# Linear attention and a mixture of experts on one core: query rows copied by DMA and transposed through an fp32r view, tail keys stacked, and a new order table

## The chip, the core and the metric

The kernel runs on one core of a Trainium2 chip. Its engines are TensorE (PE; its weight loads are listed apart as PEld), VectorE (DVE), ScalarE (ACT), GpSimd (POOL) and SyncE (SP), which here only issues DMAs. Each engine works through its own instructions in the order in which they stand; semaphores hold an instruction back until its operands are there. The metric is device time in microseconds for one execution, the median of several.

## The reference

For every batch and head, queries and keys are projected to 128 features, shifted by the row's largest absolute value, and turned into 256 features by exp(x) and exp(-x). Linear attention follows, and then one expert of eight for each token (4608 tokens of 512 numbers):

```python
def phi(x):
    proj = np.einsum('bhsd,df->bhsf', x, w_phi)
    proj = proj - np.max(np.abs(proj), axis=-1, keepdims=True)
    return np.concatenate([np.exp(proj), np.exp(-proj)], axis=-1)
q_p, k_p = (phi(q), phi(k))
kv = np.einsum('bhsf,bhsd->bhfd', k_p, v)
z = np.sum(k_p, axis=2)
num = np.einsum('bhsf,bhfd->bhsd', q_p, kv)
den = np.einsum('bhsf,bhf->bhs', q_p, z)[..., None] + 1e-06
attn = num / den                      # 8 batches, 8 heads, 576 rows, 64 columns
...
logits = x @ w_gate                   # x: attn as 4608 tokens x 512
expert_idx = np.argmax(logits, axis=1)
...
h = np.maximum(xe @ w1[e], 0.0)       # the tokens xe of expert e
out[mask] = gate_w[mask, None] * (h @ w2[e])
```

## The kernel before

**Units.** Attention runs in 16 units. A unit holds two batches (`bb`) and two heads (`hh`). The 576 rows of a batch are four chunks of 128 rows and a tail of 64; the tails of the two batches share chunk 8, batch 0 in partitions 0 to 63 and batch 1 in 64 to 127. `PIECES` (line 208) is the order of the chunks in a unit.

**Precision.** Products that must be exact to fp32 are made of fp32r operands split in two: a high part (`xh`, `kh`, `vh`, `wh`, `hh`) and the low rest (`xl`, `kl`, `vl`, `wl`, `hl`). Three matmuls, high by high, low by high, high by low, give one product. ScalarE mostly makes the high parts, VectorE and GpSimd the low ones.

**The steps of a unit.** `load` (line 234) brings `xr`, `project_steps` (257) makes the projections `ps_proj`, three matmuls of 256 columns for each chunk. `project_max` and `project` (282) take the row's maximum and write the shifted projection `t`, both on VectorE. For keys, `k_features` makes `e`, and `k_high`, `k_low` (301, 307) split it into `kh` and `kl`. For queries, `q_turn_steps` (315) transposes `t` on TensorE against the identity into `pt`, in fp32, 18 transposes of 128 by 128 in a unit, and `q_features` makes `qp` (the tail: `qz`) out of `pt`. `kv_steps` (367) sums keys by values into `pk`; the `v` tiles carry a column of ones, so that z comes with it (65 columns of weights). `CHUNKS` (205) is the order of the chunks in that sum. The tail's `v` rows are loaded twice over with zeros in the other batch's half, so that one 128-row product takes only its own batch's 64 rows. `fold_steps` makes `pf`, copied to `kf`; `num_steps` makes `pn`, numerators, denominators and logits in one, as fp32 matmuls (each recorded as two passes); `normalize` divides, and the rows go to `x_dram` by `store_steps` (213).

**The order.** `unit_items` (509) gives each step a name, `LETTERS` maps a name to a letter, and the strings `HEAD`, `GROUP` and `TAIL` (939 to 966) list the letters of all units in one sequence, which all engines and the DMA queue keep (`InOrder`, line 50, while it is on). Line 1002 reads them: `HEAD`, one `GROUP` and `TAIL`. The last 51 steps (`nums`) are issued later, among the first expert products.

**The experts.** Tokens are sorted by expert into 43 blocks of 128 (at most 41 of them run here). `block_of` and `tokens_of` (1022) place them, `gather_rows` (908) fetches a block's rows `xg` from `x_dram` by indirect DMA, `x_parts` (1128) transposes them on TensorE into `px`, four fp32 transposes for each block, and splits them. 17 pairs of blocks go through `pair_first` (`pm`, 256 columns) and `pair_second` (`po`, 512 columns), then single blocks through `first_product`, `h_parts` (four fp32 transposes `pht`) and `second_product`. The weights of the next block are loaded and split meanwhile (`raw`, `wh`, `wl`).

**Memory.** Tiles come from pools that open and close as on a stack. The pool `hold` has `xrow`, `qp` and `qz`; it is closed by `mid.close()` (1256), among the first expert products.

Of the kernel before, what the change touches and what calls it, by code (L numbers as in the profile page):

```python
# [19 lines left out]
P = 128  # L20
# [47 lines left out]
def tile_linear_attention_moe(  # L68
# [18 lines left out]
    ident = keep.tile([P, P], F32, name="ident")  # L87
    make_identity(nc, ident)
# [24 lines left out]

    w_bd = const.tile([P, 2 * F], F32, name="w_bd")
# [8 lines left out]
    V.memset(one20, 0.0)  # L123
    V.memset(one20[:, 0 : 2 * NC - 2], 1.0)
    V.memset(one20[0:D, 2 * NC - 2 : 2 * NC], 1.0)
    V.memset(one20[D:P, 2 * NC : 2 * NC + 2], 1.0)
# [22 lines left out]
    fold_parts += [lambda h=h: G.tensor_copy(fold[:, h, 0 : D + 1], ident[0 : D + 1, 0 : D + 1]) for h in range(H)]  # L149
# [27 lines left out]
    sel_p = rt.tile([P, NTILE, P], BF16, name="sel_p")  # L177
# [27 lines left out]
    CHUNKS = ((8, 0, 1, 2, 3), (4, 5, 6, 7, 8))  # L205
# [95 lines left out]
    def k_high(st, c0, n):  # L301
        m = 2 * n
        kh = kvp.tile([P, m, 2, F], F32R, name="kh", tag=f"kh{n}", bufs=3 * n - 1)
        A.copy(kh, st["e", c0][:, 0:m])
        st["kh", c0] = kh

    def k_low(st, c0, n):
        m = 2 * n
        kh = st["kh", c0]
        kl = kvp.tile([P, m, 2, F], F32R, name="kl", tag=f"kl{n}", bufs=3 * n - 1)  # L310
# [56 lines left out]
    def kv_steps(st, bb):  # L367


        def step(hh, i, c, j):  # L370
            vh, vl = v_tiles[st["u"] % 2]
            if (hh, i, j) == (0, 0, 0):
                st["pk", bb] = ps_kv.tile([P, 2, 2 * F], F32, name="pk", tag="pk")
            n = D if j == 1 else D + 1
            c0 = c if c == 8 else c - c % 2
            s0 = 2 * (c - c0)
# [3 lines left out]
                st["kl" if j == 2 else "kh", c0][:, s0 + hh].rearrange("p s f -> p (s f)"),  # L380
                start=(hh, i, j) == (0, 0, 0),
                stop=(hh, i, j) == (1, 4, 2),
# [6 lines left out]
            for j in range(3)  # L389
# [119 lines left out]
    def unit_items(st):  # L509
# [11 lines left out]
        for x in "kq":  # L521
            for c, n in PIECES:
# [405 lines left out]
    for g in range(NG):  # L928
# [9 lines left out]
    }  # L938
    HEAD = (
        "a0gb20B000000c0e212ahjd2g2ikk2jfjl2bk2D2n222m2pFKoKcssgtjje2haK22dMbjijjOqjljjuujfjjjhSSnATilkpkkkkn"  # L940
        "kGrckkkqkmkeuuuukopuurAjjjjCjjssslqsuEuuumuuutuunuuurapjjjjjjoduuuuqluufuuuunJJvJsuuLHrsBJwNsJJJJJJP"
        "JLJJJJwQsLwwICuNuuupuuNuuuukxkktJJkyUyyqRUgkkyEmyPUUuuyoUUyryaQsssysJJJtJJJLJJJJycULRyuuPuNuuuuuNuuu"
        "uuQuuuyUeKKPKKKKkkMUkUvkURkAUQkUwUUwUDmUwRUUhwOUUyUUoyUUPyxUsszsszyFzUKtKKUzyUKUyQiUbKKKKMKKVKKSyMcU"
        "SyUUOSWUSOWRSTGSSSjjjjjTljjjjnUWUlUpjjjejjnjqWUUXUpUKKlKbYUKrUYdUKUnYUqKfUYMUUYUpjjOUYUjrUAYCUjjUYqu"
        "jjjljjjjUdYluUEYuUnYuUYnuVuyuupfyauuWukkuHWruBkkkkkkkqWumIWumuyupuyXuyouyussoqySyukzrkgkzkkzkuCYSzum"
        "(YSyuZyouySyrZuTZyuyZuyuytSSzSSzvYzuEuzYzTszzY(zuYsYuYBuYsYuYsY(utJYuJYuJJJLJJJJNYuLYPuJYZuNJYQ(uJJZ"
        "YPRsJYuJZkwDukZYL)sQwuFkNwuYskPwuYxRsakkktkmkkkkyumYcuyouuQyueuoyuyuZyZuyZsZyZuRAJJJu)ysJuyZsZvJZJJJ"
        "hLJJJJUwL)sswtsUNiwsUyNsUPwUUxyUUyUtUyUKzK)UzyDzUGKKKKQzKMFKKUyOUUMPySSKRKbKOKyTUKKUyQMUUyUUyOUcUyRU"
        "UyUUyUUyUVUySUySUyeUSzyzUjzjSyUTzUy(UjjbjljjjjnUWUlUpjjjynUjqjjydlSKUWUprKySKnfWUyqUKWSKXUypASrKzKKz"
        "KMKKKTYzUUzYzUzzU(YzOCUUYUYMqUEYUYSOYUjj(jUYrSajUYSVjjjjHjljjjuWlSSWTSunIW(SuYnSupWuuXYuuYuTuYukZkuZ"  # L950
        "YgdZukkkkqZkmfkkuYouumpYsskrkBkokYtukkuYqmuuYuuYouCuYruuYuuYuuYuvuYsuYsuYEusZYZuJZJsYutZuY)uJJBJLJJ"
    )
# [52 lines left out]
    run(plan[:-51])  # L1005
    V.on = A.on = G.on = T.on = SP.on = False
    early.close()
    early.close()
# [402 lines left out]
```

## Time and profile before

| | |
|---|---|
| Runs | 909.74, 910.84, 912.04 us; median 910.84 |
| The profiled execution's own time | 909.77 us |
| Its span, first to last instruction | 908.1 us |
| Mean granted TensorE clock | 0.987 of full |
| Matmul records | 6703, among them `pk` 960, `ps_proj` 864, `pt` 288, `px` 164, `pht` 56 |
| DMA moved | 102.46 MB, mean 113 GB/s |

The page of a profile gives busy time and instruction counts for each engine, a table of 40 slices, the DMA queues, the chain of work that ended last, and the costliest groups of instructions. The other views used here are the busy time of the engines in chosen stretches, a timeline of instructions (start in us, duration in us, engine, line, operation, output<-inputs, shape, count), and the waits (who waited for whom, sum, times, longest). Where a helper issues all instructions, their line is 59, and the tile names tell them apart. "mean ns" is the duration of one instruction from its start to its end; neighbouring matmuls overlap.

### The profile page before, as it was taken

Reading aid. Unit: us, or ns where it says so; the run is one execution under the profiler, and the core shown is the slowest. Engines: PE = TensorE matmul, PEld = TensorE weight load, DVE = VectorE, ACT = ScalarE, POOL = GpSimd, SP = SyncE. Lnnn points to the kernel's source line nnn. Section 1 sums busy time; section 2 is a strip of 40 time slices with the busy share of each in tenths; the row PEclk is TensorE's granted clock in tenths of the full one; section 3 lists DMA queues with packets and bytes.
Section 4 is the critical chain, followed back from the end, with each engine's and each line's share of the span. In section 5 each row is a group of like instructions: output and inputs, shape, how many; then the busy total and the mean of one; then the engine's idle time right before and its main releaser. Section 6 shows DMA issues by size and latency. Waiting matters only on the chain. (4 is left out here: it accounts for less than half of the span.)

```text
span 908.1 us, 18331 instructions
## 1 busy us (share of the span) xinstructions
PE 882.9 (97%) x6703; PEld 824.9 (91%) x6703; DVE 589.5 (65%) x1075; ACT 611.2 (67%) x954; POOL 487.3 (54%) x332
## 2 busy tenths in 40 slices
PE   8999999999999999999999999999999999999994
PEld 6999999999999999998889999999999999987883
DVE  7777788787877788868754444444444444457950
ACT  7987888887898778844745555555555555568951
POOL 6976666776695677632543333333333333337641
PEclk8999999999999999999999999999999999999997
DMA  5243333333333341251342253522434634653100
GB/s 171 89 130 109 109 108 99 88 96 108 109 91 93 101 109 54 87 199 21 101 163 70 94 163 116 163 70 87 139 125 132 219 118 141 228 206 120 46 24 16
DMA packets 64621, 102.46 MB, mean 113 GB/s; under 512 B 10702, under 2 KB 28622, under 8 KB 64528
## 3 DMA queue, kind: packets, MB, share of 16 engines
q1 hardware_dynamic: 57136, 80.31, 28.4%
q0 software_dynamic: 6720, 20.80, 7.4%
q8 instruction: 54, 0.88, 0.4%
q14 instruction: 39, 0.32, 0.1%
q10 hardware_dynamic: 672, 0.15, 0.1%
HBM read 136.81 MB, written 20.26 MB: 173 GB/s over the span
## 5 line engine op out<-in xcount | busy, mean ns | idle before, releaser
L59 DVE TENSOR_TENSOR wl<-raw,wh 128x1024 fp32r<-128x1024 f32 x138 | 184.6, 1350 | 139.9 <-ACT wh L59 135.6
L59 ACT CAST wh<-raw 128x1024 fp32r<-128x1024 f32 x184 | 191.2, 1050 | 94.3 <-PE po L59 67.3
L59 POOL TENSOR_TENSOR wl<-raw,wh 128x1024 fp32r<-128x1024 f32 x46 | 113.4, 2470 | 172.2 <-ACT wh L59 167.0
L59 PE MATMUL pn<-kf,qp 128*128 128x73 f32 x1024 | 167.2, 251 | 0.2 <-DVE kf L59 0.2
L59 PE MATMUL pm<-xh,wh 128*128 128x256 f32 x544 | 154.6, 284 | 1.5 <-DVE hl L59 1.5
L59 PE MATMUL pm<-xl,wh 128*128 128x256 f32 x544 | 154.9, 285 | 1.2 <-DVE xl L59 1.2
L59 PE MATMUL pm<-xh,wl 128*128 128x256 f32 x544 | 154.7, 284 | 0.0
L59 PEld LDWEIGHTS pn<-kf,qp 128*128 128x128 f32 x1024 | 154.1, 189 | 0.5 <-DVE kf L59 0.4
L59 PE MATMUL po<-wh,hh 128*128 128x512 f32 x328 | 131.4, 401 | 0.3 <-ACT hh L59 0.3
L59 PE MATMUL po<-wl,hh 128*128 128x512 f32 x328 | 128.6, 392 | 0.0
L59 PE MATMUL po<-wh,hl 128*128 128x512 f32 x328 | 128.0, 391 | 0.6 <-DVE hl L59 0.6
L59 POOL TENSOR_TENSOR xl<-xr,xh 128x512 fp32r<-128x512 f32 (+2 forms) x63 | 91.6, 1456 | 61.0 <-ACT xh L59 57.3
L59 POOL TENSOR_TENSOR kl<-e,kh 128x1024 fp32r<-128x1024 f32 x47 | 112.7, 2406 | 20.0 <-ACT kh L59 10.9
L59 DVE TENSOR_REDUCE mx<-ps_proj 128x4 f32<-128x512 f32 (+1 forms) x160 | 99.9, 630 | 26.0 <-PE ps_proj L59 25.1
L59 PEld LDWEIGHTS pm<-xh,wh 128*128 128x128 f32 x544 | 104.9, 193 | 4.2 <-DVE hl L59 1.7
L59 PEld LDWEIGHTS pm<-xl,wh 128*128 128x128 f32 x544 | 104.9, 193 | 4.1 <-DVE xl L59 1.7
L59 PEld LDWEIGHTS pm<-xh,wl 128*128 128x128 f32 x544 | 104.8, 193 | 0.0
L59 DVE TENSOR_TENSOR t<-ps_proj,mx 128x512 f32<-128x512 f32 (+1 forms) x160 | 99.5, 634 | 5.5 <-ACT e L59 0.9
L59 PE MATMUL pk<-kh,vh 128*65 128x256 f32 x320 | 98.1, 307 | 0.5 <-ACT kh L59 0.5
L59 PE MATMUL pk<-kl,vh 128*65 128x256 f32 x320 | 97.7, 305 | 0.1
L59 PE MATMUL pk<-kh,vl 128*64 128x256 f32 x320 | 97.6, 305 | 0.0
L59 POOL DMA_INDIRECT out<-ob,sidx x41 | 44.5, 1086 | 91.1 <-ACT ob L59 81.2
(201 smaller groups left out, 2006.1 us busy)
## 6 DMA issues: line engine op xcount, KB each, us to landing
raw<-w SPq DMA_DIRECT2D x184, 512.0 KB
vt<-vv SPq DMA_DIRECT2D x15, 640.0 KB
x_dram<-xrow SPq DMA_DIRECT2D x30, 256.0 KB
xr<-qT SPq DMA_DIRECT2D x15, 320.0 KB
xr<-kT SPq DMA_DIRECT2D x15, 320.0 KB
xr<-kT SPq DMA_DIRECT2D x17, 256.0 KB
xr<-qT SPq DMA_DIRECT2D x17, 256.0 KB
x_dram<-xrow SPq DMA_DIRECT2D x32, 32.0 KB
```

The costliest lines, as they stand in the source:

```text
L59: m = f(*a, **kw)
```

## The change

- `q_move` is new: after `project` has written a query piece `t`, SyncE copies it by DMA into a second SBUF tile `tq` (two buffers). `q_turn_steps` transposes `tq` through an fp32r view, by the new helper `turn`, against an identity kept as fp32r. `x_parts` uses `turn` too, on `xg`, which a DMA wrote already. `h_parts` stays in fp32.
- `k_stack_steps` is new: four DMAs in a unit build two tiles `ka`, one for each batch, with the high parts of the batch's 64 tail keys in one half of the partitions and the low parts in the other. `kv_steps` then needs two products for a tail and head instead of three (with `vl` and with `vh`). For it the host puts the tail's `v` rows into both halves instead of zeros, and the ones in `one20` are set everywhere. The tail chunk comes third instead of first in the first batch's sum.
- `HEAD`, `GROUP`, `TAIL` and `LETTERS` are new, with letters for the copies; `GROUP` is read twice, and `nums` has 45 steps.
- The tail pieces of `kh` and `kl` have one buffer instead of two. The identity is built in the memory of `sel_p` and cast on VectorE. `bsel` and the small tiles of `block_of` and `experts_of` move to a pool `spots`, opened after `mid.close()`.

```diff
-    ident = keep.tile([P, P], F32, name="ident")
-    make_identity(nc, ident)
+    ident_r = keep.tile([P, P], F32R, name="ident_r")
+    ident = ident_r.bitcast(F32)
...
+    sel_p = rt.tile([P, NTILE, P], BF16, name="sel_p")
+    eye = sel_p[:, 0:2].rearrange("p a b -> p (a b)").bitcast(F32)
+    make_identity(nc, eye)
...
+    V.tensor_copy(ident_r, eye)
...
-    CHUNKS = ((8, 0, 1, 2, 3), (4, 5, 6, 7, 8))
+    CHUNKS = ((0, 1, 8, 2, 3), (4, 5, 6, 7, 8))
...
-        kh = kvp.tile([P, m, 2, F], F32R, name="kh", tag=f"kh{n}", bufs=3 * n - 1)
+        kh = kvp.tile([P, m, 2, F], F32R, name="kh", tag=f"kh{n}", bufs=4 * n - 3)
...
+    def k_stack_steps(st):
+
+        def step(b, i):
+            if i == 0:
+                st["ka", b] = kvp.tile([P, 2, 2, F], F32, name="ka", tag=f"ka{b}", bufs=2)
+            own, other = (slice(D * x, D * x + D) for x in (b, 1 - b))
+            dst, src = (other, "kl") if i else (own, "kh")
+            return SP.dma_start(st["ka", b][dst], st[src, 8].bitcast(F32)[own])
+
+        return [lambda a=(b, i): step(*a) for b in range(2) for i in range(2)]
+
+    def q_move(st, c0, n):
+        m = 2 * n
+        st["tq", c0] = work.tile([P, 4, F], F32, name="tq", bufs=2)
+        SP.dma_start(st["tq", c0][:, 0:m], st["t", "q", c0][:, 0:m])
+
+    def turn(dst, src):
+
+        return T.transpose(dst.bitcast(F32R), src.bitcast(F32R), ident_r)
...
-            return T.transpose(st["pt", c0][:, i, :], st["t", "q", c0][:, i, :], ident)
+            return turn(st["pt", c0][:, i, :], st["tq", c0][:, i, :])
...
+            if c == 8:
+                keys = st["ka", bb].bitcast(F32R)[:, hh]
+            else:
+                c0 = c - c % 2
+                keys = st["kl" if j == 2 else "kh", c0][:, 2 * (c - c0) + hh]
...
-            for j in range(3)
+            for j in ((1, 0) if c == 8 else range(3))
...
-    plan = [queues[c].pop(0) for c in HEAD + 1 * GROUP + TAIL]
-    nums = plan[-51:]
+    plan = [queues[c].pop(0) for c in HEAD + 2 * GROUP + TAIL]
+    nums = plan[-45:]
...
-            T.transpose(px[:, k, :], xg[:, k * P : (k + 1) * P], ident)
+            turn(px[:, k, :], xg[:, k * P : (k + 1) * P])
...
+    spots = late.enter_context(tc.tile_pool(name="spots", bufs=1, side="right"))
+    bsel = spots.tile([P, NTILE, NB], BF16, name="bsel")
```

What the new table does shows on two queues. TensorE before, at a place where the transposes `pt` of one unit stand among the products `pk`, `pf` and `pn` of others:

```order
L59 MATMUL pk<-kh,vh_166 65x256
L59 MATMUL pf<-fold,kvT 128x73
L59 MATMUL pt<-ident,t 128x128 x2
L59 MATMUL pf<-fold,kvT 128x73
L59 MATMUL pt<-ident,t 128x128
L59 MATMUL pk<-kh,vl_168 64x256
L59 MATMUL pf<-fold,kvT 128x73
L59 MATMUL pt<-ident,t 128x128
L59 MATMUL pk<-kl,vh_166 65x256
L59 MATMUL pn<-kf,qp 128x73
```

TensorE after, at the like place in the middle of attention:

```order
L59 MATMUL pn<-kf,qp 128x73
L59 MATMUL pt<-ident_r,tq 128x128 x4
L59 MATMUL pk<-kh,vl_166 64x256
L59 MATMUL pk<-kl,vh_164 65x256
L59 MATMUL pf<-fold,kvT 128x73
L59 MATMUL pk<-kh,vh_164 65x256
L59 MATMUL pn<-kf,qp 128x73
L59 MATMUL pk<-kh,vl_166 64x256
L59 MATMUL pf<-fold,kvT 128x73
```

The four transposes of a piece, which stood one or two at a time, now stand in a row with a `pk` product behind them: of the 288, 52 stood ahead of another `pt` before, 199 do now. Nearly every `pf` and `pn` has a `pk` or a `ps_proj` behind it, as before.

SyncE before, in the middle of attention (loads `xr` and `vt`, stores `x_dram`):

```order
L59 DMA xr<-kT 128x640
L59 DMA x_dram<-xrow 64x128
L59 DMA vt<-vv 128x1280
L59 DMA xr<-qT 128x640
L59 DMA x_dram<-xrow 128x4x128
L59 DMA xr<-qT 128x512
```

SyncE after, in a like stretch:

```order
L59 DMA tq<-t 128x512
L59 DMA x_dram<-xrow 64x128
L59 DMA vt<-vv 128x1280
L59 DMA xr<-qT 128x640
L59 DMA tq<-t 128x512
L59 DMA tq<-t 128x256
L59 DMA xr<-kT 128x640
L59 DMA ka<-kh 64x512
L59 DMA xr<-qT 128x512
L59 DMA ka<-kl 64x512
L59 DMA tq<-t 128x512
```

The five copies `tq` and the four copies `ka` of a unit stand in the same queue as its loads and stores, some right behind a load of `v`.

More of the change, by code (lines that the diff above doesn't have):

```diff
@@ L148, in tile_linear_attention_moe @@
     fold_parts = [lambda: G.memset(fold, 0.0)]
-    fold_parts += [lambda h=h: G.tensor_copy(fold[:, h, 0 : D + 1], ident[0 : D + 1, 0 : D + 1]) for h in range(H)]
+    fold_parts += [lambda h=h: G.tensor_copy(fold[:, h, 0 : D + 1], eye[0 : D + 1, 0 : D + 1]) for h in range(H)]
     def load_gate():
@@ L309, in k_low @@
         kh = st["kh", c0]
-        kl = kvp.tile([P, m, 2, F], F32R, name="kl", tag=f"kl{n}", bufs=3 * n - 1)
+        kl = kvp.tile([P, m, 2, F], F32R, name="kl", tag=f"kl{n}", bufs=4 * n - 3)
         eng = G if c0 in (4, 6) or (c0 == 0 and st["u"] > 0) else V
@@ L379, in step @@
                 (vl if j == 1 else vh)[:, 2 * (c + (bb if c == 8 else 0)) + hh, 0:n],
-                st["kl" if j == 2 else "kh", c0][:, s0 + hh].rearrange("p s f -> p (s f)"),
+                keys.rearrange("p s f -> p (s f)"),
                 start=(hh, i, j) == (0, 0, 0),
-                stop=(hh, i, j) == (1, 4, 2),
+                stop=(hh, i, j) == (1, 4, 0 if c == 8 else 2),
             )
@@ L529, in unit_items @@
                     at(("kl", c), k_low, st, c, n)
+                    if c == 8:
+                        line(("ka",), k_stack_steps(st))
                 else:
+                    at(("tq", c), q_move, st, c, n)
                     line(("t", c), q_turn_steps(st, c, n))
@@ L944, in tile_linear_attention_moe @@
[L944 to L948, printed above, removed]
@@ new lines, in tile_linear_attention_moe @@
+        "ssEsgqnwwSowSpJJrwAuJxJ[JJtLJJJyNuyLSqkySkNkyuPkrkkJJCmJJJJQuuoussDsu}suLut[KKKKEKNKyuPyMuJJuFuaJOJc"
+        "JJyuL]yQueJbyuNJyTuJJyUJRjAJycUyRLu}yPuyzuNyujjzsuQzjjjjjljsuezPunUUUlUj}jjjjnQjbUUUURUjjdjjjjUURlUP"
+        "UsUuUlu}sUuUtnuUUUUnUKKvKfKKKQUwMUwUwhUwRSASSxSjjjjyVUypUyUyTUyOUyiUy]UqyUypUW{UWUyUWqUyUrWGUyUyXrpU"
+        "yzUzySzSS{SyTUzy(UYUYqUYUYUYupYrUYuy{UYquYUYuYUyrVuyuHYzuzWuzWzzu{Wzzu(WzuYXuIjYuCjZKYZluKKYuZ(KKKYZ"
+        "CuMYuYEungYuYuOYpukkkY]EumJBJJquo(uYLu[JJJNaJJrJPuJLJJJJJQuNuuudu}uLuuvJJJRJPJJssSfNSSSuuutuLukkkTkk"
@@ new lines, in tile_linear_attention_moe @@
+        "PkkNkkkYumYQukkkokkkYQumRY[uw}uZwoDuwuwZuZYuYuZYx)uFPYuYuYuY}QuRs[sssuJaYtuJuZRJkZJyZvUZkZyZZUh)yZU3"
+        "yUJkJkkckiyLssssUUtm)wUyUNwUwUoyPUkkkk[ekkwGcUmyUyQUx)yUoyebUyU3yUKyURK4zAK34yUjMy[ssszsOjjtUzU]jjjz"
+        "j3y3U5j5ylUy3Uny5Uj7pUjljjjjqjssnsSSsDUU{UrUTjj7jjFljVjUUUltyUyUnybUpy7UnyUK{KKKpKKKKMKKKKyq7UMyUyUO"
+        "WqUrWUzOW]UWd{UzyXUyzUyU6666z666666(y3Ufpy3UyUyU4Uj{y5rSS]SS4UjAU5jKjzKTjzK5zjKzKzYzzu(qK5zluYuYMu5Y"
+        "4uYnuY5SVSSSOu(uKT5KKKK]WurWpuKWuMYuWCuYOuYquYX(uYEuYuCYuk]HSSSSkYruBkZYZumTJYuZJJuYou4uZYL[uYuN4IYu"
@@ new lines, in tile_linear_attention_moe @@
+        "JJJJ4JJJJLJJJvJSSSLSuduuuuNTs5sugYuNYufJtJYukPkkkkkP5YaumYuYEuYoQuYuQwZ}uZkRk[kJJJB4JZRkkkwZLu)Pwuwm"
+        "uYuYDxuY}uNYQuFYouYssPssu[uYuRYautJJuJky}ZUQJZkyZUZZyZUZy)vZURJkhJkkLkssssUymUtwU}yNU)wUiwocUkkkkPk["
+        "kyUmwUycUxyUoyQUyeU)yUyG4UKyUKzK4yzRUMbjsszs[sjytUOjUUzUl]yUjnjyUpeyUyUjqjjjjjVljAjjj{ssrDssSSUUtUnF"
+        "UUUylUyTUjjjnpjbjjyUly{UKpKKnKKKyUMyqUKKKOKKKyqUMry]UWU{zWOdUWUWzUzyUyUzyX(UfpyUyUyUy{qUrSS]SSUjAyTU"
+        "jUzrjKzjYzVuzKzYzzuH(YzuYujKjKKClKIYSSSSMuuT(WuYnuWuWOpuKKKKK]KYEguCMWuYquXYu(OYuYEBu"
@@ L988, in tile_linear_attention_moe @@
+        "UyUKKQKyUKKyUMySSSSyzOTUyUyzU]yzUyUzyUyUyUyUKKKKKKKKMKRKKKyUMySSSSyOTUyUyO]UyURVyzUzyzUyUzyUyUyUWzU("
+        "zWUzWzzUWzz]UUzXU((UUUU(YUYUYUYUYUYUYUYUYUYUYSVYSSSSSSTWSWWWTYXYYZYZYZYYZYYYYYYYYYYZYZYZYYZY)YYZZZZZ"
+        "ZZZ)))"
     )
@@ L1001, in tile_linear_attention_moe @@
             queues.setdefault(letters[st["u"] % 2], []).append(f)
-    plan = [queues[c].pop(0) for c in HEAD + 1 * GROUP + TAIL]
-    nums = plan[-51:]
+    plan = [queues[c].pop(0) for c in HEAD + 2 * GROUP + TAIL]
+    nums = plan[-45:]
     V.on = A.on = G.on = T.on = SP.on = True
-    run(plan[:-51])
+    run(plan[:-45])
     V.on = A.on = G.on = T.on = SP.on = False
@@ L1018, in tile_linear_attention_moe @@
         nc.sync.dma_start(raw_view(k), w_piece(lead_reg, k))
-    bsel = rt.tile([P, NTILE, NB], BF16, name="bsel")
     def block_of():
-        si_t = sg.tile([P, NTILE, E], F32, name="si_t")
-        at = sg.tile([P, NTILE], I32, name="at")
+        si_t = spots.tile([P, NTILE, E], F32, name="si_t")
+        at = spots.tile([P, NTILE], I32, name="at")
         V.tensor_tensor(si_t, onehot, spot.unsqueeze(1).to_broadcast([P, NTILE, E]), op=ALU.mult)
@@ L1027, in block_of @@
             V.tensor_reduce(at, si_t, axis=AX.X, op=ALU.add)
-        late_at = sg.tile([P, NTILE], I32, name="late_at")
-        turn = sg.tile([P, NTILE], I32, name="turn")
+        late_at = spots.tile([P, NTILE], I32, name="late_at")
+        turn = spots.tile([P, NTILE], I32, name="turn")
         V.tensor_scalar(turn, at, 6, 63, op0=ALU.arith_shift_right, op1=ALU.bitwise_and)
@@ L1033, in block_of @@
         V.tensor_single_scalar(at, at, 63, op=ALU.bitwise_and)
-        bi = sg.tile([P, NTILE], F32, name="bi")
+        bi = spots.tile([P, NTILE], F32, name="bi")
         V.tensor_tensor(bi, blk, turn, op=ALU.is_ge)
@@ L1054, in tokens_of @@
         V.tensor_scalar(gidx, pp, -1.0, 0.0, op0=ALU.add, op1=ALU.max)
-        emp = sg.tile([P, NB], F32, name="emp")
+        emp = spots.tile([P, NB], F32, name="emp")
         V.tensor_scalar(emp, pp, 0.5, BIG, op0=ALU.is_lt, op1=ALU.mult)
@@ L1059, in experts_of @@
     def experts_of():
-        ends = sg.tile([1, 2, E], F32, name="ends")
+        ends = spots.tile([1, 2, E], F32, name="ends")
         G.tensor_tensor(ends[:, 0], first[0:1], paired[0:1], op=ALU.add)
@@ L1063, in experts_of @@
         V.tensor_reduce(nblk, ends[:, 1], axis=AX.X, op=ALU.max)
-        eg = sg.tile([1, 2, NB, E], F32, name="eg")
+        eg = spots.tile([1, 2, NB, E], F32, name="eg")
         places = ((first[0:1], ends[:, 0], 0, 2 * NPAIR), (start[0:1], ends[:, 1], 2 * NPAIR, NB))
@@ L1246, in tile_linear_attention_moe @@
     weights(0, 1)
-    run(nums[16:36])
+    run(nums[16:30])
     run(r1[:1])
-    run(nums[36:])
+    run(nums[30:])
     weights(0, 3)
@@ L1384, in rows @@
         tail = a[..., 4 * P :, :].transpose(0, 2, 1, 4, 3, 5).reshape(NG * NPR, P, 2, D)
-        res = np.zeros((NG * NPR, P, 2 * NC + 2, D), a.dtype)
+        res = np.empty((NG * NPR, P, 2 * NC + 2, D), a.dtype)
         res[:, :, 0:16] = main
-        res[:, 0:D, 16:18] = tail[:, 0:D]
-        res[:, D:P, 18:20] = tail[:, D:P]
+        for b in range(2):
+            half = tail[:, D * b : D * b + D]
+            res[:, :, 16 + 2 * b : 18 + 2 * b] = np.concatenate([half, half], axis=1)
         return res
```

64 lines of the change are left out of this document (18 added, 46 removed), and 5 rows, old and new, of the table LETTERS.

## The prediction

> **What bounds the kernel now.** I read the page's engine totals first, then each engine's busy time by stretches.
>
> ```profile
> span 908.1 us, 18331 instructions
> PE 882.9 (97%) x6703; PEld 824.9 (91%) x6703; DVE 589.5 (65%) x1075; ACT 611.2 (67%) x954; POOL 487.3 (54%) x332
> ```
>
> ```profile
> core 0: us, PE busy (x) PEld busy (x) DVE busy (x) ACT busy (x) POOL busy (x), PEclk, DMA share, GB/s
> 30.00:60.00 30.00, 30.00 (x280) 29.91 (x279) 23.14 (x39) 27.91 (x44) 25.33 (x14) 1.00 0.35 105
> 150.00:210.00 60.00, 58.17 (x550) 57.79 (x548) 48.43 (x102) 53.35 (x98) 44.95 (x29) 1.00 0.36 105
> 240.00:270.00 30.00, 30.00 (x290) 29.89 (x288) 23.85 (x61) 27.25 (x52) 25.77 (x19) 1.00 0.29 83
> 30.00:390.00 360.00, 354.96 (x3340) 352.16 (x3338) 285.51 (x654) 298.25 (x533) 257.20 (x157) 1.00 0.35 101
> 480.00:800.00 320.00, 320.00 (x2086) 293.14 (x2085) 154.10 (x164) 172.24 (x219) 123.94 (x84) 1.00 0.42 137
> ```
>
> Attention fills 30 to 390 us and the expert products 480 to 800 us. TensorE is busy for 355 of 360 us in the first and without a gap in the second, at the full granted clock (1.00). Next comes ScalarE with 298 us, 83%. "Busy" alone proves little, since matmuls overlap; so I asked what TensorE waits for.
>
> ```profile
> engine line waited for: us in total, times, longest us
> PE ps_proj L59 <- DVE t L59: 5.0, 5, 1.8
> PE pm L59 <- DVE hl L59: 1.5, 1, 1.5
> ```
>
> The longest entry is 5 us in the whole run. So TensorE's own stream sets the end, and an edit is worth what it takes out of that stream, less the waits it adds.
>
> The duration of one matmul is mostly pipeline. What it costs the stream is the distance from the end of the one before to its own end, read from the timeline (start, duration):
>
> ```profile
> 569.92 0.28 PE L59 MATMUL pm<-xl,wh 128*128 128x256 f32 x1
> 570.04 0.28 PE L59 MATMUL pm<-xh,wl 128*128 128x256 f32 x1
> 570.16 0.60 PE L59 MATMUL px<-ident,xg 128*128 128x128 f32 x4
> 570.52 0.48 PE L59 MATMUL po<-wh,hh 128*128 128x512 f32 x1
> ...
> 304.86 0.34 PE L59 MATMUL pn<-kf,qp 128*128 128x73 f32 x2
> 305.00 0.31 PE L59 MATMUL pk<-kl,vh 128*65 128x256 f32 x1
> 305.15 0.28 PE L59 MATMUL pk<-kh,vh 128*65 128x256 f32 x1
> 305.27 0.34 PE L59 MATMUL pn<-kf,qp 128*128 128x73 f32 x2
> ...
> 306.08 0.28 PE L59 MATMUL ps_proj<-w_hi,xh 128*128 128x256 f32 x1
> 306.20 0.22 PE L59 MATMUL pn<-kf,qp 128*128 128x73 f32 x1
> ```
>
> An fp32r matmul of 256 columns ends 0.12 us after its predecessor (570.20, 570.32), a `pk` product 0.11 to 0.12 (305.20, 305.31, 305.43). Four fp32 transposes end at 570.76, so each costs 0.11: as much for 128 columns as an fp32r product for 256. An fp32 `pn` product runs as two passes of 73 columns. The first ends 0.06 after the matmul ahead (306.36, 306.42), both together 0.18 (305.43, 305.61). So the second costs 0.12 for the same 73 columns: its weights could not load behind so short a pass. That is the hidden price of a short matmul: the next weight load sticks out, and a load of 128 columns occupies about 0.11 us.
>
> **The change part by part.**
>
> *Tail keys.* High and low parts of a tail now lie in one tile, so a tail takes two products for each head instead of three. In 16 units, with two batches and two heads each, that is 64 of 960 `pk` products less, at 0.118 us (the 0.11 and 0.12 above): **-7.6 us**.
>
> *Transposes.* 288 of `pt` and 164 of `px` become fp32r; the 56 of `pht` stay.
>
> ```profile
> L59 PE MATMUL po<-wh,hl 128*128 128x512 f32 x328 | 128.0, 391 | 0.6 <-DVE hl L59 0.6
> L59 PE MATMUL pm<-xh,wl 128*128 128x256 f32 x544 | 154.7, 284 | 0.0
> L59 PE MATMUL px<-ident,xg 128*128 128x128 f32 x164 | 24.8, 273 | 0.4 <-DMA xg<-x_dram,gidx 0.4
> ```
>
> No fp32r transpose stands in this trace, so I bound it. From 512 to 256 columns an fp32r product falls from 391 to 284 ns, 0.42 ns a column; at 128 columns it would last 230 ns, 43 less than the fp32 transpose's 273, so 0.109 becomes 0.066. If fp32r streams at exactly half the cost of fp32, it is 0.054. At the bad end the view changes nothing and it stays 0.109. I take 0.060, between the two fp32r rows: 49 ns less.
>
> What follows may now show its weight load: 110 less 60 leaves 50 ns, if that load has 128 columns. The load rows (mean ns) tell which do:
>
> ```profile
> L59 PEld LDWEIGHTS pm<-xh,wl 128*128 128x128 f32 x544 | 104.8, 193 | 0.0
> L59 PEld LDWEIGHTS pk<-kl,vh 128*65 128x65 f32 x320 | 44.2, 138 | 0.5 <-DVE kl L59 0.3
> L59 PEld LDWEIGHTS px<-ident,xg 128*128 128x128 f32 x164 | 19.1, 141 | 1.0 <-DMA xg<-x_dram,gidx 0.8
> ```
>
> A `pk` load of 65 columns takes 55 ns less than one of 128, and the load of a transpose is as short as that. So a transpose or a `pk` behind a transpose hides its load; `ps_proj`, `pn`, `pf` and `po` don't. In the new order 199 of the 288 `pt` stand ahead of another `pt` and 47 ahead of a `pk`; 39 stand ahead of a long load. `pt`: 288 x 0.049 - 39 x 0.050 = **-12.2 us**. `px`: 164 x 0.049, less 41 groups x 0.050 for the product behind each: **-6.0 us**, in the stage where nothing but TensorE is full.
>
> The Trainium skill, "TensorE: Matmul & The Clock Gate", section "LDWEIGHTS (loading the stationary operand)", gives a load as columns / 1.2 ns, 107 for 128 columns. The second `pn` pass agrees (0.12). By that figure a run of transposes would be bound by loads whatever its type; the `px` load row (141 against 193 ns) speaks against it for transposes. The page's "Back-to-back issue gap" has 81 ns for 128 columns with their loads; by that the two terms would be some 10 us instead of 18 (my estimate).
>
> *Copies.* SyncE issues 80 copies `tq` (64 of 256 KB, 16 of 128 KB) and 64 of `ka` (128 KB). Each `tq` adds a wait: TensorE's next `pt` stands behind it, and on TensorE everything behind that `pt`. No DMA from SBUF to SBUF is in this trace. The nearest:
>
> ```profile
> 0.81 0.40 SPq L59 DMA_DIRECT2D xr<-kT  x1
> ...
> 3.56 0.31 DVE L59 CAST xh<-xr 128x128 fp32r<-128x128 f32 x1
> ...
> x_dram<-xrow POOLq DMA_DIRECT2D x2, 256.0 KB, 3.3
> ```
>
> A load of 64 KB was used 2.75 us after its issue began; a store of 256 KB landed after 3.3. At the prices above, the order table has between a copy and its first `pt` 3.6 us of TensorE work in the middle, in units 3 to 15 never under 2.86. Summing what sticks out over all 80: 3 us at 2.7 us a copy, 9 at 3.3, 23 at 3.7. I take 2.75, as these are reads that nothing in DRAM delays: **+3 us**, nearly all of it in units 0 to 2, where loads stand thick.
>
> The added issues cost SyncE 144 x some 0.4 us, where it has been waiting:
>
> ```profile
> SPq L59 <- POOL xl L59: 136.4, 47, 9.1
> SPq L59 <- DVE lgc L59: 96.6, 28, 9.9
> ```
>
> A copy queued behind such a wait would be late; in the new order loads and stores stand among the copies (the rows of SyncE in the section on the change), each at about the place where what they wait for is done. The bytes: 18.4 + 8.4 MB more, in a stage that moves 101 GB/s at a DMA share of 0.35; over some 340 us that is 180 GB/s and a share of about 0.6. The `ka` copies have 5 us and more before their first product and cost nothing. Single-buffered tail `kh` and `kl` are free again one copy later, against a unit of some 22 us. Identity, memsets and the `spots` tiles lie beside the first loads or beside full TensorE work: 0.
>
> *Cover.* Attention loses 19.8 us of TensorE work, so ScalarE's 298 us stand against about 341: 87%. From 30 to 60 us it had 27.91 of 30 and TensorE lost nothing; less 5% leaves 28.4. Just enough.
>
> **Sum.** -7.6 - 12.2 - 6.0 + 3 = -22.8 us. The profiled execution took 909.8 us (its span 908.1): 887.0. The median of the runs is 1.1 above it: **888 us**.
>
> **Rivals.**
> - *The fp32r view does not make transposes cheaper*, because the load bounds a run of them (0.11 each within a run, only the first of the 89 runs of `pt` gaining 49 ns, 39 times given back). Then -7.6 - 2.4 + 3 leaves 904. For it: the `pn` pass. Against: the load row of `px`. 0.07. At 81 ns a transpose, by that page's sentence, it is 896: 0.05.
> - *ScalarE becomes the bound* where it has over 26.5 of 30 us (30 to 60, 150 to 210, 240 to 270: a third of attention). Those stretches keep their length: 6.6 of 19.8 us lost, 895. For it: 27.91 of 30. 0.12.
> - *The copies stall TensorE: slower.* It decides between 3.7 and 3.8 us a copy, where what sticks out eats the 25.8 us gained; at 4.0 it sums to 43 us, 928. A `v` load of 640 KB just ahead in the same queue, or a SyncE wait, could do it. Against: 2.75 us measured, and a queue at 0.6. 0.07.
>
> **How the numbers follow.** The forecast (881 to 893: 0.054 to 0.066 a transpose, copies at 2.7 to 3.0 us) has 0.67; 0.02 lies below. The range 878 to 900 takes in also the cases at 895 and 896, and leaves out 904 and 928: about 0.8. A measurement tells 0.3% from no change, 2.7 us. Faster: 0.67 + 0.02 + 0.07 + 0.05 + 0.12, less a little for copies near their limit: 0.90. Slower 0.07, within 0.03.
>
> **What would show it.** Right: `px` x4 rows of about 0.41 us instead of 0.60; `pk` 896 times; the last `pt` some 17 us earlier and the stretch of expert products 6 us shorter; TensorE's waits on `tq` at 3 us, mostly before 60 us. Wrong: `px` rows unchanged (the view); waits of TensorE on `tq` of over 10 us, or waits on `kh`, `e` or `qp` (ScalarE).

## The result, and the profile after

The changed kernel takes 919.74 us, the median of eight runs (914.45 to 926.25); the kernel before took 909.91 beside it (906.96 to 912.04). The ratio is 1.0104, with a 95% interval of 1.0068 to 1.0140. So it is slower by 1%, where 2.5% faster was forecast. The profiled execution of after took 914.93 us with a span of 913.2, against 909.77 and 908.1 before: 5.1 us more of span, which is what the stages below add up to. That execution is the second shortest of the eight; of the 9.8 us between the medians the stages explain about half.

The page of the changed kernel, its totals:

```profile
span 913.2 us, 18579 instructions
PE 873.3 (96%) x6639; PEld 811.0 (89%) x6639; DVE 587.3 (64%) x1073; ACT 611.0 (67%) x954; POOL 487.8 (53%) x332
DMA packets 81262, 129.73 MB, mean 142 GB/s; under 512 B 13006, under 2 KB 32974, under 8 KB 81168
```

TensorE has 64 matmuls less and is busy for 9.6 us less, and yet the span is longer: work went, and waiting came. The busy time by stages of after (columns as in the prediction):

```profile
0.00:30.00 30.00, 24.11 (x146) 19.79 (x147) 22.53 (x45) 21.16 (x37) 22.05 (x41) 0.89 0.71 221
30.00:390.00 360.00, 344.67 (x3238) 337.68 (x3237) 279.16 (x647) 296.74 (x530) 258.17 (x157) 0.99 0.55 165
480.00:800.00 320.00, 320.00 (x2092) 292.50 (x2091) 156.21 (x166) 174.17 (x221) 122.04 (x83) 1.00 0.41 133
```

From 30 to 390 us TensorE is idle for 15.3 us (5.0 before), and the DMA share rose from 0.35 to 0.55. The page's waits, after, say for what:

```profile
engine line waited for: us in total, times, longest us
PE pt L59 <- DMA tq<-t: 13.3, 13, 3.2
PE ps_proj L59 <- DVE t L59: 2.9, 4, 1.0
PE pm L59 <- DVE hl L59: 2.5, 1, 2.5
PE ps_proj L59 <- ACT xh L59: 2.2, 2, 1.2
```

The transposes wait for the new copies: 13 times, 13.3 us in all. The timeline of after shows where they fall; these are the five longest of the 13 (in brackets the idle time and what ended it):

```profile
116.07 0.54 PE L59 MATMUL pt<-ident_r,tq 128*128 128x128 f32 x4 [1.88 <-DMA tq<-t]
140.91 0.88 PE L59 MATMUL pt<-ident_r,tq 128*128 128x128 f32 x6 [1.53 <-DMA tq<-t]
238.11 0.88 PE L59 MATMUL pt<-ident_r,tq 128*128 128x128 f32 x6 [1.47 <-DMA tq<-t]
314.63 0.72 PE L59 MATMUL pt<-ident_r,tq 128*128 128x128 f32 x6 [3.23 <-DMA tq<-t]
340.03 0.93 PE L59 MATMUL pt<-ident_r,tq 128*128 128x128 f32 x6 [1.06 <-DMA tq<-t]
```

All five lie beyond 110 us, in the steady part of attention. Of the 13 only one, of 0.6 us, lies ahead of 60 us, where the prediction expected most.

Behind two of these waits, and at one more place in attention, TensorE's granted clock (third column from the right) falls to half for 3.4 us. I call that a spell at half clock; it costs 1.7 us:

```profile
142.20:145.60 3.40, 3.40 (x20) 3.40 (x19) 1.89 (x3) 3.38 (x8) 0.00 (x0) 0.51 0.49 118
275.40:278.80 3.40, 3.40 (x21) 3.40 (x19) 1.45 (x8) 2.49 (x3) 2.48 (x2) 0.51 0.84 236
316.30:319.70 3.40, 3.40 (x20) 3.40 (x19) 1.38 (x2) 3.40 (x7) 0.00 (x0) 0.50 0.00 0
```

What SyncE issued ahead of the wait at 116 us, in the timeline of after:

```profile
106.53 0.48 SPq L59 DMA_DIRECT2D tq<-t  x1
107.10 1.30 SPq L59 DMA_DIRECT2D vt<-vv  x1
108.46 0.47 SPq L59 DMA_DIRECT2D x_dram<-xrow  x1
109.01 0.54 SPq L59 DMA_DIRECT2D xr<-qT  x1
109.65 0.37 SPq L59 DMA_DIRECT2D xr<-kT  x1
110.12 1.72 SPq L59 DMA_DIRECT2D tq<-t  x2
```

The copy at 106.53 is used 3.7 us later, without a wait. The two issued from 110.12 on come behind a `v` load (640 KB), a store and two loads; TensorE gets the first of them at 116.07, 6.0 us after its issue. The trace also has the single DMA packets, 128 of 2 KB for such a copy. A copy with nothing ahead of it (issued at 132.02) moves them from 1.1 to 2.0 us after its issue. The first packet of the copy issued at 110.12 moves at 113.31, 3.2 us after the issue, when all packets of the `v` load ahead of it and 134 of the 256 of the two `xr` loads are through.

For the comparisons below I cut attention at the same work in every kernel: units 3 to 15, from the end of the 163rd to the end of the 811th `ps_proj` product (54 a unit, so twelve units). These four rows are those products, the first two in the timeline of before:

```profile
70.44 0.28 PE L59 MATMUL ps_proj<-w_hi,xh 128*128 128x256 f32 x1
365.26 0.28 PE L59 MATMUL ps_proj<-w_hi,xh 128*128 128x256 f32 x1
```

and the other two in that of after:

```profile
71.48 0.28 PE L59 MATMUL ps_proj<-w_hi,xh 128*128 128x256 f32 x1
368.63 0.28 PE L59 MATMUL ps_proj<-w_lo,xh 128*128 128x256 f32 x1
```

| stage of the profiled execution | before | after | difference |
|---|---|---|---|
| up to unit 3 | 70.7 | 71.8 | +1.1 |
| units 3 to 15 | 294.8 | 297.1 | +2.3 |
| from there to the last `pn` | 39.4 | 39.8 | +0.4 |
| last `pn` to first `pp` (the handover to the experts) | 21.7 | 24.9 | +3.2 |
| the rest | 481.5 | 479.6 | -1.9 |

In the rest one wait differs among the kernels with the new table. Six of the eight profiles of such kernels (no_copy and others below) have the first of these rows there, after and v_on_act the second:

```profile
PE pm L59 <- DVE xl L59: 3.6, 1, 3.6
PE pm L59 <- DVE xl L59: 1.4, 1, 1.4
```

With the longer wait comes a spell at half clock, and the rest takes 483.5 to 484.7 us instead of some 480. So the median execution of the changed kernel may well have it too, which would be the other half of the 9.8 us; no profile of after shows it.

### The profile page after: what moved, and what is told of

Read it like the earlier page. It is cut to its first block, busy times and chain, and to the rows that moved or that the text cites. A ratio compares the mean times of both kernels' runs of the same rounds, so it can differ in the third digit from the quotient of the medians.

```text
span 913.2 us, 18579 instructions
## 1 busy us (share of the span) xinstructions
PE 873.3 (96%) x6639; PEld 811.0 (89%) x6639; DVE 587.3 (64%) x1073; ACT 611.0 (67%) x954; POOL 487.8 (53%) x332
## 5 line engine op out<-in xcount | busy, mean ns | idle before, releaser
L59 PE MATMUL pn<-kf,qp 128*128 128x73 f32 x1024 | 162.0, 254 | 0.7 <-ACT qp L59 0.7
L59 POOL TENSOR_TENSOR kl<-e,kh 128x1024 fp32r<-128x1024 f32 x47 | 114.8, 2443 | 62.9 <-ACT kh L59 43.6
L59 POOL TENSOR_TENSOR xl<-xr,xh 128x512 fp32r<-128x512 f32 (+2 forms) x63 | 88.9, 1416 | 34.3 <-ACT xh L59 29.7
L59 ACT ACTIVATE e<-t 128x512 f32<-128x512 f32 (+1 forms) x160 | 84.3, 588 | 23.9 <-DVE t L59 12.9
L59 PE MATMUL ps_proj<-w_hi,xh 128*128 128x256 f32 x288 | 84.0, 298 | 5.2 <-DVE t L59 2.9
L59 ACT ACTIVATE qp<-pt 128x512 f32<-128x512 f32 x128 | 69.1, 594 | 28.6 <-PE pt L59 28.3
```

Of the source, the lines that this page charges most:

```text
L59: m = f(*a, **kw)
```

## The experiments

The first four ran on one chip beside eleven runs of the kernel before, which took 914.89 us there (910.29 to 917.07). Each is the changed kernel with one part of it undone or moved. Two theories stood against each other in them: the copies cost the time (behind loads, or by their wait as such), or the new order does so by itself.

### no_copy: the new order, no query copies

```diff
-        t = work.tile([P, 4, F], F32, name="t", bufs=4)
+        t = work.tile([P, 4, F], F32, name="t", bufs=6)
...
-        m = 2 * n
-        st["tq", c0] = work.tile([P, 4, F], F32, name="tq", bufs=2)
-        SP.dma_start(st["tq", c0][:, 0:m], st["t", "q", c0][:, 0:m])
+        st["tq", c0] = st["t", "q", c0]
...
-            return turn(st["pt", c0][:, i, :], st["tq", c0][:, i, :])
+            return T.transpose(st["pt", c0][:, i, :], st["tq", c0][:, i, :], ident)
```

> The changed kernel and its order table, but without the copies tq: query pieces are transposed in fp32 straight from t (six buffers of t instead of four and two of tq). Theory Q (the copies wait behind loads in the same DMA queue and TensorE waits for them): TensorE's 13.3 us of waits on tq go, with them two of the half-clock spells of 1.7 us each; the fp32 transposes cost 5.5 us more; 902 to 906 us. Rival O (the new order loses the time by itself, the copies only show it): 912 us or more, with the waits moved to other tiles.

Measured: 905.76 us, ratio 0.9903 (0.9868 to 0.9939). Units 3 to 15 take 284.7 us, 10.1 less than before. So the order, the stacked keys and the fp32r `px` are a gain together, and it is the copies, as they stand in the queue, that turn it into a loss.

### rounded: fp32r transposes without a copy

```diff
-        t = work.tile([P, 4, F], F32, name="t", bufs=6)
+        t = work.tile([P, 4, F], F32R if x == "q" else F32, name="tr" if x == "q" else "t", tag="t", bufs=6)
...
-            return T.transpose(st["pt", c0][:, i, :], st["tq", c0][:, i, :], ident)
+            return T.transpose(st["pt", c0][:, i, :].bitcast(F32R), st["tq", c0][:, i, :], ident_r)
```

(against no_copy)

> The changed kernel without the copies, but with fp32r transposes: VectorE writes the query's t as fp32r, which rounds it (the output differs by that rounding). Theory Q: no wait on copies, transposes at their new cost: 895 to 900 us. Rival O: 910 us or more. Against no_copy it gives the worth of the fp32r view for pt alone: 5.5 us by the distances in the changed kernel's trace (theory S: a run of fp32r transposes is bound by its weight loads at 0.085 us each and shows 0.07 us of the next load), 12 us by the prediction.

Measured: 904.98 us, ratio 0.9899 (0.9864 to 0.9934); units 3 to 15 take 282.7 us. That is not the 895 to 900 us expected. The view for `pt` is worth 2.0 us in twelve units of these two profiles, and in the medians 0.8, which these runs can't tell from nothing. The copies were made for that view; this kernel leaves out exactness, since VectorE rounds the queries as it writes them.

### copy_fp32: the copies, but fp32 transposes

```diff
-            return turn(st["pt", c0][:, i, :], st["tq", c0][:, i, :])
+            return T.transpose(st["pt", c0][:, i, :], st["tq", c0][:, i, :], ident)
```

> The changed kernel with the copies, but pt transposed in fp32 out of tq; px stays fp32r. Theory S: the stream grows by 5.5 us and part of that is cover for late copies, so 915 to 922 us, little different from the changed kernel. If the view were worth the predicted 12 us for pt: 922 to 930 us.

Measured: 923.23 us, ratio 1.0099 (1.0061 to 1.0138); units 3 to 15 take 298.1 us, 13.4 more than no_copy with the same transposes. By its time it would fall among the 922 to 930 us that were given for a view worth 12 us, but the kernel before was 5 us slower on this chip too; by ratio it stands where after does (1.0104), so beside the copies the view shows no worth. Its waits:

```profile
PE pt L59 <- DMA tq<-t: 12.8, 8, 2.8
```

### loads_behind: loads moved behind the copies

Among the steps of the new table, loads of `xr` and `v` up to 40 steps ahead of a copy are issued behind it (not in the first and last 400 steps):

```diff
+        if steps[i][0] in "[]":
+            lo = max(400, i - 40)
+            loads = [x for x in steps[lo:i] if x[0] in "gGaAbB"]
+            if loads:
+                rest = [x for x in steps[lo:i] if x[0] not in "gGaAbB"]
+                steps[lo : i + 1] = rest + [steps[i]] + loads
...
```

> The changed kernel, where a load of xr or v that stands up to 40 steps of the table ahead of a copy tq is issued behind it (all but the first and last 400 steps). Theory Q: the waits on tq fall from 13.3 us to under 4 us and the time to 898 to 905 us. Rival O: about as the changed kernel, 914 to 922 us. If the loads then come too late, waits on xr appear on ScalarE instead.

Measured: 907.01 us, ratio 0.9924 (0.9899 to 0.9949); units 3 to 15 take 283.7 us. By ratio that is what no_copy has, though all copies are made, with the same bytes; the wait is all but gone:

```profile
PE pt L59 <- DMA tq<-t: 1.2, 2, 0.8
```

So it is not the copy as such, nor the wait for one undisturbed, but a copy in company of loads. In after the packets ran in the order of SyncE's queue, the copy's behind the loads'. That leaves open what helps: is it enough to take load and copy into different queues, or are they in each other's way there too?

The next four ran beside 29 runs of the kernel before (910.21 us, 905.82 to 912.29).

### v_on_act: the v load from another queue

```diff
-        SP.dma_start(st["vt"], vv[u])
+        A.dma_start(st["vt"], vv[u])
```

> The changed kernel, with the v load of a unit (640 KB) issued from ScalarE's DMA queue instead of SyncE's, at the same place of the order: the same bytes at about the same time. Theory Q (a copy is late because it stands behind the load in the same queue, first in first out): the late copies behind a v load come about 2 us earlier, TensorE's waits on tq fall from 13.3 us to half or less, last pn some 6 to 8 us earlier, total 910 to 913 where the changed kernel has 920. Rival B (the copy is late because load and copy share the DMA engines, whatever their queue): waits on tq stay at 10 us or more and the time stays. Possible side effect: ScalarE holds back its own work where the v tile is not free yet.

Measured: 911.43 us, ratio 1.0008 (0.9985 to 1.0031). Units 3 to 15 take 288.3 us, 8.8 less than after, but the waits didn't fall to half:

```profile
PE pt L59 <- DMA tq<-t: 10.5, 10, 2.3
```

Neither theory's line came out whole: the waits say that the DMA engines are shared, the time that something was gained. In the timeline the copies behind a `v` load are now mostly in time, and the one issued beside it is late instead. The copy issued at 111.70 us is an example: nothing is ahead of it in SyncE's queue, the `v` load is issued at the same time in ScalarE's, and the copy's first packet moves at 115.04, when 101 of the load's 128 packets (from 112.69 on) are through. Of the 8.8 us, the waits explain 3.3 (11.8 to 8.5 in this stage), and 5.1 are the three spells at half clock of after, which v_on_act doesn't have there. In turn it takes 76.7 us up to unit 3, 4.9 more than after.

### tq_on_act: the copies in a queue of their own

```diff
-        SP.dma_start(st["tq", c0][:, 0:m], st["t", "q", c0][:, 0:m])
+        A.dma_start(st["tq", c0][:, 0:m], st["t", "q", c0][:, 0:m])
```

> The changed kernel, with the query copies tq issued from ScalarE's DMA queue instead of SyncE's; loads, stores and ka copies stay where they are. With the v load moved to ScalarE's queue instead, the waits on tq only fell from 13.3 to 10.5 us: the copy issued before the load then came late, the two behind it came earlier. So two theories are left. Q (the place in the queue): alone in their queue the copies stand behind no load; the waits on tq fall below 4 us, units 3 to 15 take 284 to 287 us (297.1 in the changed kernel, 284.8 without copies). B (load and copy share the DMA engines whatever their queue): waits on tq of 8 us or more stay, units 3 to 15 take 288 us or more. Against both: ScalarE issues 80 DMAs more and may hold back its own casts where t is late; waits of TensorE on xh, qp or e would show that.

Measured, beside 20 runs of the kernel before (912.04 us, 910.01 to 916.94): 921.23 us, ratio 1.0089 (1.0060 to 1.0118); units 3 to 15 take 293.6 us. Theory Q's numbers (waits below 4 us, 284 to 287 us) are missed widely. The waits grew over the whole run; in units 3 to 15 they are 11.2 us, near the 11.8 of after, and the growth lies ahead of them and behind:

```profile
PE pt L59 <- DMA tq<-t: 19.0, 15, 3.3
```

The clearest place, in the timeline of this kernel; the two issues first, then the transpose:

```profile
110.09 0.49 ACTq L59 DMA_DIRECT2D tq<-t  x1
...
110.29 0.33 SPq L59 DMA_DIRECT2D vt<-vv  x1
...
117.26 0.75 PE L59 MATMUL pt<-ident_r,tq 128*128 128x128 f32 x4 [3.31 <-DMA tq<-t]
```

The copy is issued 0.2 us ahead of the load, alone in its queue, and TensorE has it only 7.2 us later. Its packets tell why: 121 of the 128 are through by 112.32, the other seven move only from 113.92 on, when 109 of the load's 128 (from 112.21 on) are through. A place in the queue can't explain that, so the theory that the queue alone makes copies late falls. Load and copy move through the same DMA engines, whichever queue they come from, and TensorE waits for the last packet. On the engines the Trainium skill says the same: "DMA: Bandwidth & Descriptors", section "Issuing engines are not separate DMA queues", has all issuers end up on the same 16 engines, interleaved. These waits agree.

### px_only and px_double: the price of a transpose

px_only is the kernel before with the fp32r view for `px` alone; px_double issues each of its runs twice:

```diff
-            T.transpose(px[:, k, :], xg[:, k * P : (k + 1) * P], ident)
+            T.transpose(px[:, k, :].bitcast(F32R), xg[:, k * P : (k + 1) * P].bitcast(F32R), ident_r)
...
-        for k in range(KD):
+        for k in [*range(KD), *range(KD)]:
```

> The kernel before, with the four px transposes of a block through the fp32r view and nothing else of the change. Theory R (a transpose costs 60 ns only where it is the first of a run, 79 to 84 ns behind another transpose, and the 128-column load behind the run sticks out by some 70 ns): 41 groups save 436 - 369 = 67 ns each, 2.8 us, ratio about 0.997, px x4 rows of 0.45 us, waits of TensorE as before. The prediction's step (0.060 each, 50 ns sticking out): 6.0 us less, ratio 0.9934.

> px_only with each run of four px transposes issued twice, eight in a row into the same tile: the same result, 164 transposes more. It measures the cost of a transpose inside a run by itself. Theory R: 164 x 0.079 to 0.084 = 13 to 14 us above px_only. The prediction's 0.060 each: 9.8 us above. If the weight load bounds a run as in fp32 (0.109): 18 us above.

Measured: px_only 911.99 us, ratio 1.0019 (1.0003 to 1.0035); px_double 921.03, ratio 1.0136 (1.0112 to 1.0160). As whole times neither fits: px_only should have been 2.8 us faster, px_double lies 9.0 above it instead of 13. The expert stage alone is free of waits, so it can be read from the timelines. The runs of two blocks 27 blocks apart, in before:

```profile
476.75 0.60 PE L59 MATMUL px<-ident,xg 128*128 128x128 f32 x4
477.10 0.48 PE L59 MATMUL po<-wh,hh 128*128 128x512 f32 x1
...
797.63 0.60 PE L59 MATMUL px<-ident,xg 128*128 128x128 f32 x4
```

in px_only:

```profile
481.16 0.46 PE L59 MATMUL px<-ident_r,xg 128*128 128x128 f32 x4
481.46 0.47 PE L59 MATMUL po<-wh,hh 128*128 128x512 f32 x1
...
800.50 0.45 PE L59 MATMUL px<-ident_r,xg 128*128 128x128 f32 x4
```

and in px_double:

```profile
480.35 0.80 PE L59 MATMUL px<-ident_r,xg 128*128 128x128 f32 x8
...
808.67 0.80 PE L59 MATMUL px<-ident_r,xg 128*128 128x128 f32 x8
```

These are 320.88, 319.34 and 328.32 us. The view saves 1.54 us in 27 blocks, 57 ns a block; four more transposes add 8.98, or 83 ns each. That is the price inside a run. And the weight load behind the run does stick out: the `po` product ends 0.23 us after the run in before (477.58 against 477.35) and 0.31 in px_only (481.93 against 481.62), by rows rounded to 0.01. So 41 blocks save 2.3 us.

What became of it in px_only? At these blocks it is 4.4 us behind before (481.16 against 476.75), though nothing there was changed but how the identity is made. Part of it can be seen. These windows hold the same wait of TensorE for `t`, in before:

```profile
174.80:178.20 3.40, 1.65 (x15) 1.68 (x16) 2.87 (x5) 2.18 (x6) 0.49 (x2) 1.00 0.66 193
178.20:181.60 3.40, 3.40 (x35) 3.40 (x33) 2.54 (x7) 3.28 (x7) 1.25 (x1) 1.00 0.30 83
```

and in px_only:

```profile
174.80:178.20 3.40, 1.58 (x16) 1.55 (x15) 2.87 (x4) 2.18 (x6) 0.58 (x1) 1.00 0.75 216
178.20:181.60 3.40, 3.40 (x21) 3.40 (x19) 1.81 (x4) 2.45 (x6) 1.27 (x1) 0.50 0.27 80
```

The same idle time, but in px_only the granted clock (third column from the right) is 0.50 behind it, and 21 matmuls are done instead of 35. Why px_only has more such spells (another comes at 840 us, one at 417 lasts twice as long) these runs don't tell: one profile of each is too few. The same holds for stages: units 3 to 15 are the same code in before, px_only and px_double and take 294.8, 297.4 and 296.2 us. So a difference of 2 or 3 us between two profiles of these units shows little by itself.

### stack_only and stack_late: the stacked keys in the old order

Both have the table of before, no query copies, fp32 `pt`, fp32r `px` and the stacked tails; stack_late leaves the tails of units 0 and 1 as before.

```diff
+        if c0 == 8 and st["u"] > 1:      # stack_only: if c0 == 8
+            run(k_stack_steps(st))
...
-            for i, c in enumerate(CHUNKS[bb])
+            for i, c in enumerate((0, 1, 8, 2, 3) if bb == 0 and 2 <= st["u"] < 16 else CHUNKS[bb])   # stack_only: < 15
```

> The order table of before, with the stacked tail keys (two products for each tail and head, 64 of 960 pk products less) and the fp32r px, but no query copies: pt in fp32 straight out of t. In units 2 to 14 the tail stands third in the first batch's sum, in the others first as before. Theory: -7.6 us from 64 products at 0.118 and -2.8 us from px, about 899.5 where before has 910, ratio 0.9886; the handover from the last pn to the last pp stays near the 24.4 us of before, since the old table gives it (26 to 28 with the new table). Rival: the stack's copies are late in the units with the tail first, and the gain falls to 5 us. If it is faster than no_copy (0.9903) the new table has no worth of its own.

> stack_only, with the tails of units 0 and 1 as before (three products, v rows with zeros in the other batch's half), so that no product waits for the stacks while the pipeline fills, and unit 15 with its tail third. In stack_only units 0 and 1 lost 8.4 us at once (waits on ka of 5.5 us and two half-clock windows), units 3 to 15 gained 7.0. Theory: the gain stays and the loss goes: unit 2 ends its first projections at about 45.5 us as before, units 3 to 15 take 288 us, total 6 to 9 us less than before, ratio 0.990 to 0.9935. Rival: the loss comes from the extra DMA issues of the whole start and stays: ratio 1.00 or above.

Measured: stack_only 912.77 us, ratio 1.0045 (1.0026 to 1.0064), where 0.9886 was forecast. It gains 7.0 us in units 3 to 15 (287.8), and had lost 8.2 before them, most of it in two waits for the stacks (of 5.5 and 2.0 us):

```profile
PE pk L59 <- DMA ka<-kl: 8.9, 3, 5.5
```

stack_late measured 911.24 us, ratio 0.9991 (0.9972 to 1.0011): no such wait, but units 3 to 15 take 291.8 us, with a spell of 6.8 us at half clock at 176 us behind a wait of over 2 us; another stands at 374, behind these units. So the forecast of 6 to 9 us failed here too. The two have the same products in units 3 to 15, and their gains there, 7.0 and 3.0 us, lie on either side of what was computed (5.7); over the whole run it was lost again to waits and half clock in the old order.

### no_copy_again

> no_copy once more, beside stack_late and more runs of the kernel before: does the gain of 0.9903 (0.9868 to 0.9939), measured against a kernel before that ran at 914.9 us there, hold against one that runs at 910? By stages it should: units 3 to 15 took 284.8 us against 294.8, of which 1 to 3 us came back at the start and in the handover. Expected 0.989 to 0.993; 0.997 or above would say that part of the first ratio came from the other runs' half-clock windows.

Measured, on the chip of stack_late: 905.81 us, ratio 0.9920 (0.9890 to 0.9950); units 3 to 15 take 284.8 us, within 0.1 of no_copy. It holds. This is the change without its query copies; rounded (0.9899) and loads_behind (0.9924) can't be told from it. Against stack_late beside it, it takes 5.4 us less. About 1 us of that are the 8 `pk` products that stack_late has more; the rest is the new order, with its two more buffers of `t`: a worth that the prediction never priced.

## Why the prediction was wrong

**The copies** are the step that failed. Its words: 80 copies at 2.75 us each against what the order table leaves them, "+3 us, nearly all of it in units 0 to 2". Measured in units 3 to 15, where it expected next to nothing: 297.1 us with copies and 282.7 in rounded, which has the same fp32r transposes and none: 14.4 us. The waits there are 11.8 us, the three spells at half clock 5.1 (rounded has none there); other waits are 2.7 us shorter in turn. Two of the three spells come directly behind a wait for a copy, the third behind other waits. The step that was wrong is one price for all 80 copies. 2.75 us was not too little for an undisturbed one: its packets are through 2.0 us after the issue, and TensorE's waits ended as little as 0.4 us after the last packet. But an average share of 0.6 was taken for room (it came out at 0.55), though a copy meets a load of 640 KB at its own moment. The copies that TensorE waited for came 3.6 to 7.1 us after their issue, where the order mostly leaves some 3.6; there were 13 of them, not quite one in a unit, and the others cost nothing. (The 18.4 MB should read 18.9, which changes nothing.)

**The rival "the copies stall TensorE"** was the right one, at 0.07. It named the `v` load "just ahead in the same queue". The load was right. The queue was half of it: in after the packets do stand behind the loads', but tq_on_act shows that another queue is no way out. Its 928 us took 4.0 us for every copy; 919.74 came of few late ones.

**Transposes of queries**, -12.2 us: 2.0 us in units 3 to 15 without copies (no_copy against rounded), 1.0 with them (copy_fp32 against after). The 0.060 us holds only at the start of a run; 0.083 holds inside, and the weight load behind a run sticks out by 70 to 80 ns, not 50. By these prices 89 x 0.049 + 199 x 0.026 - 39 x 0.070 = 6.8 us would be left over all units, some 5 in these twelve. Less than half of that was seen, and 2.0 us is within what two profiles of the same code differ by; where the rest went no run tells.

**px**, -6.0 us: the sizes again, -2.3. "`px` x4 rows of about 0.41 us" was the sign asked for; they have 0.45. That the view is cheaper was right, so the first rival (no gain, the load bounds a run) fell; the 81 ns by which it gave 896 was near the truth for the transposes alone.

**Tail keys**, -7.6 us: 896 `pk` products as forecast, and a gain in units 3 to 15 of 7.0 (stack_only) or 3.0 (stack_late), where 48 products less at 0.118 make 5.7. The size is not refuted, nor pinned down closer than that.

**ScalarE** did not become the bound: with all gains and no waits on copies (rounded), units 3 to 15 run in 282.7 us, and TensorE's longest sum of waits for ScalarE is 2.2 us in after.

**Not priced at all**: the new order itself (no_copy takes 3.1 us less than stack_only in units 3 to 15, 7.1 less than stack_late), the longer wait for `xl` in the rest (above), and the handover, 3.2 us longer in after. The handover takes 24.9 or 25.0 us in the five profiles with the new table that have one spell at half clock there, 23.3 or 23.4 in the three that have none, and 21.7 or 21.8 in the three with the old table and one such spell. So it belongs to the new table. 96 `pm` products instead of 88 stand between the last `pn` and the first `pp`, which is 1.0 us at 0.12; what makes the rest is open.

For units 3 to 15 the measured terms close by construction: -7.0 (stack), -3.1 (order), -2.0 (view), +14.4 (copies), in sum +2.3 us. With stack_late in the place of stack_only the first two would be -3.0 and -7.1. Only the copies' term stands well clear of what two profiles of the same code differ by.

## What to carry to other kernels

Before a wait for a DMA is put on the path of a full engine, look at what else is in flight at that moment in the order, not at the mean share; here a queue of its own didn't help, and moving the load did. A wait costs more than its length where the clock falls behind it. And try a change without the transfer that TensorE would wait for: here that was worth 0.8 to 1%, and the copies took back twice that until the loads were moved.

## What the hardware showed

- **Half clock after waits.** In the thirteen profiles of this study, between 45 and 880 us, a spell at half clock began during a wait of TensorE or within 4.5 us of its end in all 8 cases of a wait of 3 us or more, in 14 of 22 of 2 to 3 us, in 8 of 10 of 1.5 to 2 us, and in 5 of 82 of 0.6 to 1.5 us (a wait is the idle time in the brackets of the timeline). A spell lasts 3.4 or 6.8 us there and costs half of that. The rows of before and px_only above are the same wait with both outcomes. The Trainium skill, "TensorE: Matmul & The Clock Gate", Part 1, has a free-running window of 3413 ns; the lengths agree. The rule in its section "Why this matters for your kernels", no idle gaps over about 3 us, is too wide here: 1.5 us did it (the wait at 140.91 in after).
- **fp32r transposes** of 128 by 128 cost 83 ns in a run, fp32 ones 110, both at a granted clock of 1.00.
- **A copy of 256 KB inside SBUF** had moved its last packet 2.0 us after its issue when little else moved. With a load of 640 KB under way TensorE got it 6.0 us after its issue behind the load in the same queue (after) and 7.2 beside it in another (tq_on_act).
